# Row maxima of both heads of a pair in one product, and 64-bit weights converted with one VectorE pass

## The chip, the cores and the metric

The kernel runs on one core of a Trainium2 chip. The metric is the time of one execution in microseconds (us) on the device. A program on one core reports the time of that core. The kernel before was run three times; the median is what counts.

A core has five engines that run their own lists of instructions in order and wait for each other by semaphores: TensorE (PE, with its weight loads shown apart as PEld), VectorE (DVE), ScalarE (ACT), GpSimd (POOL) and SyncE (SP), which here only issues DMAs.

## The reference

Three layers in a row. Attention with queries averaged in pairs (4 batches, 8 heads, 1152 keys, 576 pooled queries, 64 wide):

```python
q_pool = q.reshape(B, H, S // factor, factor, D).mean(axis=3)
scores = scale * np.matmul(q_pool, k.transpose(0, 1, 3, 2))
scores = scores - np.max(scores, axis=-1, keepdims=True)
attn = np.exp(scores)
attn = attn / (np.sum(attn, axis=-1, keepdims=True) + 1e-09)
return np.matmul(attn, v).astype(np.float32)
```

Then a gated unit on 2304 tokens of 512 features, `silu(x @ w_gate) * (x @ w_val) @ w_out`, with 1536 hidden units, and a layer of eight soft experts with four slots each: a softmax of `x @ phi` over the tokens makes the slots' inputs, two layers per expert their outputs, and a softmax over the slots the result. `w_gate`, `w_val` and `w_out` arrive as 64-bit floats, all else as 32-bit floats.

## The kernel before

Attention goes in 16 steps, four batches with four pairs of heads. Of each pair the kernel forms, for every key chunk of 128 and 512 queries, the scores in a PSUM bank `st` (`unit`, lines 372 to 394): a product of `KK` and `QQ` (line 380; keys in float16 over queries in high and low float16 halves) and one of `KL` and `QH` (line 381; the keys' low halves over the queries' high ones). In two more rows of `QH` (64 and 65, against rows of 16.0 in `KL`) stand minus a query's greatest score, in a high and a low half: so the second product also takes the maximum off. ScalarE makes the exponential (line 386), GpSimd or VectorE what its high half lacks (line 393), and TensorE multiplies with the values (lines 424 to 426).

The maxima come from `row_max` (243 to 334), one head at a time: products of the high halves into banks `mx` (lines 268 and 272), and VectorE's greatest of each bank (line 288, 294, 298). In pairs 1 to 4 (`SC_STEPS`) ScalarE copies one bank of two to SBUF (280) and VectorE takes both in one scan (281) and copies its last column out (282). Then four small VectorE operations per head (300, 301, 304, 305) make the two halves. For pairs up to 6 TensorE turns them and ScalarE copies them into `QH` (327, 331, 333). From pair 7 on (`MT_STEP`) one product turns them (310), ScalarE copies them out (312), and two DMAs per head, and two more with head 1, put them in their rows (314, 320).

`split_pair` (204 to 242) makes the halves of the next pair's keys and queries and copies them by DMA to where the products want them; it is called at the start of each step for the pair of the next. `maxima` paces the row maxima: at the start of a step 18 of the 21 banks of its pair (`MXN`, `LEAD`) have been asked for, and all of head 0 must be there before the step's first scores (9), all of head 1 before its own (21).

The weights of the gated unit are converted during steps 1 to 6 (`PREP_BEG`, `PREP_END`), six pieces of 128x512 a step, 36 in all. `conv` (519 to 541) reads a 64-bit number as two words. ScalarE scales the high word as a float (532). VectorE shifts the low word (534), shifts the scaled number and joins the two (535), and joins the sign (538).

From step 4 on blocks of the gated unit (lines 602 to 607 on TensorE, 613 to 644 around it) are mixed in, three blocks are left when attention ends, and then come the experts. A scheduler sets the order on each engine, from a simulated timeline and the order of the code; what `maxima`, `prep` and `moe_work` ask for at each unit decides what it has to choose from.

Of the kernel before, what the change touches and what calls it, by code (L numbers as in the profile page):

```python
# [10 lines left out]
F16 = mybir.dt.float16  # L11
# [3 lines left out]
U32 = mybir.dt.uint32  # L15
AF = mybir.ActivationFunctionType
# [48 lines left out]
def tile_pool_attention_glu_softmoe(  # L65
# [65 lines left out]
    # places for the conversion of weights at first, for the experts' weights later  # L131
# [7 lines left out]
    # the last blocks' tokens lie apart from what is free with the attention's end  # L139
# [34 lines left out]
    def cast(what, b, p, dst, src):  # L174
        """Copies for which the scalar engine has time in the first steps."""
# [17 lines left out]
    def first_split(kd, qd, KK, KL, QQ, QH):  # L193
        """The first head with no more transfers, to begin early."""
# [9 lines left out]
    def split_pair(b, p, first=None):  # L204
# [6 lines left out]
        QH = at.tile([D + 2, 2, SQ], F16, tag="QH", bufs=2, name=f"QH{b}_{p}")  # L211
# [6 lines left out]
        # both heads of the pair at once; DMAs copy the halves to where the products want them  # L218
# [3 lines left out]
        kh = at.tile([P, S], F16, tag="kh", bufs=1, name=f"kh{b}_{p}")  # L222
        cast("k", b, p, kh[r], kr[r])
# [7 lines left out]
        heads = range(1 if first else 0, 2)  # L231
        for hd in heads:
# [10 lines left out]
    def row_max(b, p, hd):  # L243
# [12 lines left out]
        def bank():  # L256
            n_bank[0] += 1
            tg, bf = "mx", MXB
            if first and n_bank[0] % 2 or i < MX_STEPS and n_bank[0] % MX_OF == 1:
                tg, bf = "mm", MMB  # L260
            return ps(tg, [P, QT], bufs=bf, name=f"mx{b}_{p}_{hd}_{n_bank[0]}")
# [13 lines left out]
        for s in range(4):  # L275
            ts = [scores(bank(), s, c * QT, QT) for c in range(2)] if not first and i in SC_STEPS else []
            if ts:
                # while the scalar engine has time it brings a bank to SBUF, and two banks go through one scan
                w = h_tile(f"ms{b}_{p}_{hd}_{s}")[1]
                nc.scalar.copy(w, ts[0])  # L280
                nc.vector.tensor_tensor_scan(out=w, data0=ts[1], data1=w, initial=-3.0e38, op0=ALU.max, op1=ALU.max)  # L281
                nc.vector.tensor_copy(out=mp[:, s, :2], in_=w[:, QT - 1:].to_broadcast([P, 2]))
# [804 lines left out]
```

## Time and profile before

| what | before |
|---|---|
| three runs | 950.49, 954.99 and 955.86 us, median 954.99 us |
| span of the profiled execution | 951.9 us, 3.1 us below the median |
| PE busy | 843.9 us, 89% of the span |
| DVE busy | 679.5 us, 71% |
| POOL busy | 450.3 us, 47% |
| ACT busy | 365.7 us, 38% |
| DMA queue 1 | 51.5% of 16 engines |
| mean granted TensorE clock | 0.956 |

The profile is of one execution; its span runs from the first to the last instruction, and its own time is taken as that span. A busy share is a mean over stages that have different limits. So the span was cut where attention steps end (the last normalisation of a step, line 449 on five columns, begins there): 0 to 67.4 us is step 0, 67.4 to 187.9 steps 1 to 3, 187.9 to 333.2 steps 4 to 6, 333.2 to 761.4 steps 7 to 15, and the rest the last blocks and the experts. TensorE's products overlap, so its busy time is more than it would need back to back.

### The profile page before, as it was taken

The numbers are of one execution on the slowest core, as the hardware profiler recorded it, in microseconds if no ns is written. First come the engines' busy times: TensorE is split into PE (matmuls) and PEld (weight loads), VectorE is DVE, ScalarE is ACT, GpSimd is POOL, SyncE is SP. The second block draws the span as 40 slices with busy tenths as digits, with TensorE's granted clock in tenths as the row PEclk, the third lists the DMA queues.
The fourth block names the chain that finished last, engine by engine and source line by source line (L and its number), as shares of the span: only waits on it lengthen the run. The fifth ranks groups of instructions, "written<-read, shape, count | busy, mean of one in ns | idle before, by whom it ended". The sixth has DMA issues, their size and how long they took to land.

```text
span 951.9 us, 24241 instructions
## 1 busy us (share of the span) xinstructions
PE 843.9 (89%) x10071; PEld 584.5 (61%) x10071; DVE 679.5 (71%) x1266; ACT 365.7 (38%) x699; POOL 450.3 (47%) x382
## 2 busy tenths in 40 slices
PE   3887777879988779999898989998999999998897
PEld 1454454558555557767575766765777787776445
DVE  6899999998899766787867796867676343543313
ACT  2456666654555421433332434143334411212112
POOL 7555856564568830655754677265546500000100
PEclk9788998999998999999998999998999999999998
DMA  6465456564866572243523243331312189548899
GB/s 180 131 175 175 107 185 202 147 199 130 202 156 203 147 185 46 62 116 74 116 68 98 68 123 72 106 69 34 73 32 35 24 236 304 136 134 189 260 291 280
DMA packets 150070, 132.51 MB, mean 139 GB/s; under 512 B 81352, under 2 KB 118920, under 8 KB 149960
## 3 DMA queue, kind: packets, MB, share of 16 engines
q1 hardware_dynamic: 149960, 130.96, 51.5%
q8 instruction: 79, 1.29, 0.6%
q14 instruction: 31, 0.25, 0.1%
HBM read 84.10 MB, written 7.86 MB: 97 GB/s over the span
## 4 chain that ended last, share of the span: by engine, by line
PE 58%; DVE 22%; DMA 10%; issue 4%; SPq 3%; ACT 1%; POOL 0%; DVEq 0%; ACTq 0%
PE mx L268 5%; PE st L380 4%; PE st L381 4%; PE v L602 4%; PE v L607 4%; PE g L602 4%; PE v L606 4%; PE g L606 4%; PE g L607 4%; PE pv L425 2%; PE pv L424 2%; PE pv L426 2%; DVE ms L281 2%; DMA KK<-kh 2%; DVE mp L288 2%
## 5 line engine op out<-in xcount | busy, mean ns | idle before, releaser
L393 POOL TENSOR_TENSOR PL<-P 128x512 f16<-128x512 f32 (+1 forms) x295 | 330.7, 1136 | 276.2 <-ACT P L386 270.8
L386 ACT ACTIVATE P<-st 128x512 f32<-128x512 f32 (+1 forms) x336 | 189.3, 582 | 185.1 <-PE st L381 160.6
L288 DVE TENSOR_REDUCE mp<-mx 128x1 f32<-128x512 f32 x192 | 128.6, 683 | 32.4 <-PE mx L268 31.8
L268 PE MATMUL mx<-KK,QQ 128*128 128x512 f16 (+2 forms) x384 | 116.0, 353 | 39.3 <-DVE mp L288 12.3
L424 PE MATMUL pv<-VV,P 128*128 128x65 f16 x1088 | 144.6, 196 | 6.2 <-DVE x L452 6.1
L380 PE MATMUL st<-QQ,KK 128*128 128x512 f16 (+1 forms) x576 | 142.0, 297 | 5.1 <-ACT P L386 4.7
L425 PE MATMUL pv<-VV,P 128*128 128x64 f16 x1088 | 145.0, 198 | 0.0
L426 PE MATMUL pv<-VV,PL 128*128 128x65 f16 x1088 | 140.5, 195 | 1.6 <-DVE PL L393 1.5
L381 PE MATMUL st<-QH,KL 66*128 66x512 f16 (+1 forms) x576 | 140.0, 297 | 0.2
L602 PE MATMUL g<-xT,wgv 128*128 128x256 f16 x432 | 119.1, 276 | 7.1 <-DVE hs L614 6.5
L424 PEld LDWEIGHTS <-P 128*128 128x128 bf16 x1088 | 106.0, 100 | 28.3 <-issue 7.6
L602 PE MATMUL v<-xT,wgv 128*128 128x256 f16 x432 | 118.7, 275 | 0.6 <-DVE hs L616 0.5
L606 PE MATMUL g<-xT,wgv 128*128 128x256 f16 x432 | 119.0, 275 | 0.0
L607 PE MATMUL g<-xT,wgv 128*128 128x256 f16 x432 | 118.9, 275 | 0.1
L606 PE MATMUL v<-xT,wgv 128*128 128x256 f16 x432 | 118.8, 275 | 0.0
L607 PE MATMUL v<-xT,wgv 128*128 128x256 f16 x432 | 118.6, 274 | 0.0
L426 PEld LDWEIGHTS <-PL 128*128 128x128 f16 x1088 | 105.4, 101 | 20.0 <-issue 5.9
L425 PEld LDWEIGHTS <-P 128*128 128x128 bf16 x1088 | 105.3, 100 | 19.5 <-issue 6.2
L606 PEld LDWEIGHTS <-wgv 128*128 128x128 f16 x864 | 85.2, 99 | 30.1 <-issue 12.7
L602 PEld LDWEIGHTS <-wgv 128*128 128x128 f16 x864 | 85.6, 99 | 22.9 <-issue 6.2
L607 PEld LDWEIGHTS <-wgv 128*128 128x128 f16 x864 | 85.0, 99 | 18.7 <-issue 1.9
L613 ACT ACTIVATE hs<-g 128x512 f32<-128x512 f32 x54 | 32.1, 596 | 93.0 <-PE g L607 51.5
(182 smaller groups left out, 1404.3 us busy)
## 6 DMA issues: line engine op xcount, KB each, us to landing
w<-in_w SPq DMA_DIRECT2D x16, 1024.0 KB
w<-in_w SPq DMA_DIRECT2D x64, 256.0 KB
vr<-in_vP SPq DMA_DIRECT2D x16, 585.0 KB
KK<-kh SPq DMA_DIRECT2D x62, 144.0 KB
qr<-in_qT SPq DMA_DIRECT2D x15, 576.0 KB
kr<-in_kT SPq DMA_DIRECT2D x15, 576.0 KB
ro<-in_w_out SPq DMA_DIRECT2D x12, 512.0 KB
rw<-in_w_gate SPq DMA_DIRECT2D x24, 256.0 KB
```

Of the source, the lines that this page charges most:

```text
L268: nc.tensor.matmul(t, QQ[r, s * P:(s + 1) * P], KK[r, kc], start=True, stop=True)
L288: nc.vector.reduce_max(out=mp[:, s, c:c + 1], in_=t, axis=AX.X)
L380: nc.tensor.matmul(t[:, o:o + w], KK[:, k], QQ[:, q0:q0 + w], start=True, stop=False)
L381: nc.tensor.matmul(t[:, o:o + w], KL[:, k], QH[:, q0:q0 + w], start=False, stop=True)
L386: marks.append(nc.scalar.activation(P32[:, :o], t[:, :o], AF.Exp, scale=1.0 / 16.0).ins.name)
L393: eng.tensor_tensor(out=PL[:, :o], in0=P32[:, :o], in1=PH[:, :o], op=ALU.subtract)
L424: nc.tensor.matmul(dst[:, :D + 1], PH[:, q], VV[:, c, 0, :], start=first, stop=False, skip_group_check=True)
L425: nc.tensor.matmul(dst[:, :D], PH[:, q], VV[:, c, 1, :D], start=False, stop=False, skip_group_check=True)
L426: nc.tensor.matmul(dst[:, :D + 1], PL[:, q], VV[:, c, 0, :], start=False, stop=(c == NCH - 1), skip_group_check=True)
L602: mm = nc.tensor.matmul(o, w[:, 0, d, f], xh, start=(d == 0), stop=False)
L606: nc.tensor.matmul(o, w[:, 0, d, f], xl, start=False, stop=False)
L607: nc.tensor.matmul(o, w[:, 1, d, f], xh, start=False, stop=(d == ND - 1))
```

## The change

**Weights.** ScalarE does two operations per piece and VectorE one. The scaling uses the function Prelu with a slope of -2^32 for negative numbers, which leaves the sign as one more bit of the exponent; a second operation takes the top byte of the low word, divides it by 32 and writes the whole number; one VectorE pass shifts and joins. `L534` and `L538` go, a ScalarE line 546 comes.

**Row maxima.** A tile `QD` holds the high halves of a pair's queries, head 0 in rows 0 to 63 of its first half, head 1 in rows 64 to 127 of its second, zeros elsewhere. So one product of 128 columns of `QD` with the pair's keys `kh` (both heads over each other, as they were cast) gives scores of either head: nine groups of 128 queries, each every ninth column, times 1152 keys. Pair 0 keeps the way by heads (`row_max_first`). The scans are gone: every bank is one reduction. `QD` is one buffer, filled by two DMAs per pair from `qh`, and `kh` is read by the products themselves, so both can be written anew only when the last product of the pair before has read them.

**One row.** The maximum goes into one row of `QH` in one float16, and `KL` has one row of 16.0. One VectorE operation takes the greatest of nine groups at once (337), one ScalarE operation scales and rounds it (`taken_off`, 307), and one DMA of 128 rows of nine numbers writes it to `QH` (341). There are no turning products from pair 1 on, and no DMAs of `L314` and `L320`.

**Pace.** Before a step's first scores all of its pair's maxima are asked for (`MX0 + MXP * i`), and those of the next pair between 4% and 85% of the step; in step 0 from 40% to its end.

```diff
 def split_pair(b, p, first=None):
...
+        if not first:
+            for hd in heads:
+                nc.sync.dma_start(out=QD[rows[hd], hd, :], in_=qh[rows[hd], :])
...
+    def taken_off(dst, src):
+        nc.scalar.activation(dst, src, AF.Copy, scale=-1.0 / 16.0, bias=math.log(PSC))
+    NGQ = SQ // D
+    def row_max(b, p):
+        kh = KHs.pop((b, p))
+        mp = at.tile([P, NGQ, 3], F32, tag="mp", bufs=2, name=f"mp{b}_{p}")
+        R = S - 2 * QT
+        def scores(t, g, k0, kw):
+            q = QD.rearrange("p h q -> p (h q)")[:, g::NGQ]
+            nc.tensor.matmul(t, q, kh[:, k0:k0 + kw], start=True, stop=True)
+        for g in range(NGQ):
+            for c in range(2):
+                t = ps("mx", [P, QT], bufs=MXB, name=f"mx{b}_{p}_{g}_{c}")
+                scores(t, g, c * QT, QT)
+                nc.vector.reduce_max(out=mp[:, g, c:c + 1], in_=t, axis=AX.X)
+                yield
+            if g % 4 == 3 or g == NGQ - 1:
+                g0 = g // 4 * 4
+                n = g + 1 - g0
+                t = ps("mx", [P, 4, R], bufs=MXB, name=f"mx{b}_{p}_{g}_r")
+                for x in range(n):
+                    scores(t[:, x, :], g0 + x, 2 * QT, R)
+                nc.vector.reduce_max(out=mp[:, g0:g + 1, 2:3], in_=t[:, :n, :], axis=AX.X)
+                yield
+        nm = at.tile([P, NGQ], F32, tag="nm", bufs=2, name=f"nm{b}_{p}")
+        nc.vector.tensor_reduce(out=nm, in_=mp, axis=AX.X, op=ALU.max)
+        mt = at.tile([P, NGQ], F16, tag="mt", bufs=2, name=f"mt{b}_{p}")
+        taken_off(mt, nm)
+        nc.sync.dma_start(out=QHs[b, p][D:D + 1].rearrange("o h (q g) -> o (h q) g", g=NGQ), in_=mt)
+        yield
...
-        nc.scalar.mul(y, hi.bitcast(F32), sc * 2.0**-112)
+        nc.scalar.activation(y, r[:, :, 1].bitcast(F32), AF.Prelu, scale=sc * 2.0**-112, alpha=-(2.0**32))
         w = t[:, 3 * n:]
-        nc.vector.tensor_scalar(w, lo, 29, None, ALU.logical_shift_right)
+        top = r[:, :, 0].bitcast(U8)[:, :, 3]
+        nc.scalar.activation(w, top, AF.Copy, scale=1.0 / 32.0, bias=1.0 / 64.0 - 0.5)
         nc.vector.scalar_tensor_tensor(
             out=w, in0=y.bitcast(U32), scalar=3, in1=w, op0=ALU.logical_shift_left, op1=ALU.bitwise_or
         )
-        nc.vector.scalar_tensor_tensor(
-            out=w, in0=hi, scalar=1 << 31, in1=w, op0=ALU.bitwise_and, op1=ALU.bitwise_or
-        )
...
-            maxima(int(MXN * (i + f) + (LEAD if i else 9 + LEAD0 * f)))
+            if i:
+                maxima(MX0 + MXP * i + int(MXP * min(1.0, max(0.0, f - MX_BEG) / (MX_END - MX_BEG))))
+            else:
+                maxima(9 + int((MX0 - 9) * min(1.0, f / MX0_END)) + int(MXP * max(0.0, f - MX1_BEG) / (1.0 - MX1_BEG)))
```

The order that the scheduler makes of it differs in three places that matter below.

VectorE in step 1, before, while the first weights are converted (`ro` and `rw` are pieces of weights, `ms` a scan of two banks, `mp` the maxima):

```order
L535 SCALAR_TENSOR_TENSOR ro1_975<-ro1_975 128x512
L281 SCALAR_TENSOR_TENSOR ms0_2_0_1_1056<-mx0_2_0_4_1054,ms0_2_0_1_1056 128x512
L534 TENSOR_SCALAR rw0_0_1091<-rw0_0_1091 128x512
L538 SCALAR_TENSOR_TENSOR ro1_975<-ro1_975 128x512
L282 COPY mp0_2_0_1005<-ms0_2_0_1_1056 128x2
L535 SCALAR_TENSOR_TENSOR rw0_0_1091<-rw0_0_1091 128x512
L281 SCALAR_TENSOR_TENSOR ms0_2_0_2_1111<-mx0_2_0_6_1109,ms0_2_0_2_1111 128x512
L221 TENSOR_TENSOR qr1_0_1572<-qr1_0_1572 128x576
L538 SCALAR_TENSOR_TENSOR rw0_0_1091<-rw0_0_1091 128x512
L282 COPY mp0_2_0_1005<-ms0_2_0_2_1111 128x2
L281 SCALAR_TENSOR_TENSOR ms0_2_0_3_1157<-mx0_2_0_8_1155,ms0_2_0_3_1157 128x512
```

And now, in the same step:

```order
L325 TENSOR_REDUCE mp0_2_901<-mx0_2_4_0_1096 128x1
L547 SCALAR_TENSOR_TENSOR rw0_0_1056<-rw0_0_1056 128x512
L325 TENSOR_REDUCE mp0_2_901<-mx0_2_4_1_1111 128x1
L458 TENSOR_SCALAR rs0_1_0_1133<-pv0_1_0_905 128x4
L325 TENSOR_REDUCE mp0_2_901<-mx0_2_5_0_1140 128x1
L459 RECIPROCAL rs0_1_0_1133<-rs0_1_0_1133 128x4
L325 TENSOR_REDUCE mp0_2_901<-mx0_2_5_1_1150 128x1
L547 SCALAR_TENSOR_TENSOR rw0_1_1153<-rw0_1_1153 128x512
L461 TENSOR_TENSOR x320_1_0_1136<-pv0_1_0_905,rs0_1_0_1133 128x256
L325 TENSOR_REDUCE mp0_2_901<-mx0_2_6_0_1181 128x1
```

Where there stood three passes per piece and a scan with its copy, there stand one pass per piece and two reductions.

TensorE before, as it goes from step 0 to step 1 (`pv` are products with the values, `st0_1_0` the first scores of pair 1; the transposes of that pair's first maxima, `mt0_1_0`, are 26 products further up):

```order
L426 LDWEIGHTS PL0_0_15_558
L426 MATMUL pv0_0_1_502<-VV0_0_120,PL0_0_15_558 128x65
L424 LDWEIGHTS P320_0_16_583
L424 MATMUL pv0_0_1_502<-VV0_0_120,P320_0_16_583 128x65
L425 LDWEIGHTS P320_0_16_583
L425 MATMUL pv0_0_1_502<-VV0_0_120,P320_0_16_583 128x64
L268 LDWEIGHTS QQ0_1_300
L268 MATMUL mx0_1_1_6_853<-KK0_1_299,QQ0_1_300 128x512
L381 LDWEIGHTS KL1_103
L381 MATMUL st0_1_0_811<-QH0_1_301,KL1_103 128x512
```

And now, at the same place (`mx0_1_8` is the last group of pair 1's maxima, `tx` turns features of pair 0):

```order
L319 LDWEIGHTS QD_106
L319 MATMUL mx0_1_8_1_750<-kh0_1_308,QD_106 128x512
L319 LDWEIGHTS QD_106
L319 MATMUL mx0_1_8_r_771<-kh0_1_308,QD_106 128x128
L500 LDWEIGHTS xhl0_0_206
L500 MATMUL tx0_0_803<-id16_66,xhl0_0_206 64x64
L500 LDWEIGHTS xhl0_0_206
L500 MATMUL tx0_0_803<-id16_66,xhl0_0_206 64x64
L390 LDWEIGHTS KL1_103
L390 MATMUL st0_1_0_816<-QH0_1_306,KL1_103 128x512
```

The second product of the scores, which needs the row of maxima, now follows the last product of those maxima after two small ones.

SyncE before, where step 1 ends (the loads of pair 3 stand in one piece, and nothing there writes maxima):

```order
L236 DMA QQ0_3_1545<-qh0_3_1550 64x576
L237 DMA QQ0_3_1545<-ql0_3_1552 64x576
L240 DMA QH0_3_1546<-qh0_3_1550 64x576
L239 DMA KL1_103<-kl0_3_1554 64x1152
L240 DMA QH0_3_1546<-qh0_3_1550 64x576
L526 DMA ro2_1576<-in_w_out 128x1024
L526 DMA ro3_1692<-in_w_out 128x1024
L481 DMA_TRANSPOSE xT0_799<-xhl0_1_810 128x4x128
L481 DMA_TRANSPOSE xT1_801<-xhl0_1_810 128x4x128
```

And now:

```order
L247 DMA QH0_3_1484<-qh0_3_1488 64x576
L238 DMA QD_106<-qh0_3_1488 64x576 x2
L247 DMA QH0_3_1484<-qh0_3_1488 64x576
L240 DMA KK0_3_1482<-kh0_3_1486 64x1152
L341 DMA QH0_2_826<-mt0_2_1360 1x128x9
L241 DMA KK0_3_1482<-kh0_3_1486 64x1152
L240 DMA KK0_3_1482<-kh0_3_1486 64x1152
L490 DMA_TRANSPOSE xT0_799<-xhl0_1_815 128x4x128
L490 DMA_TRANSPOSE xT1_801<-xhl0_1_815 128x4x128
L241 DMA KK0_3_1482<-kh0_3_1486 64x1152
```

The DMA that writes pair 2's maxima (`QH0_2<-mt0_2`) now stands behind the two that refill `QD` for pair 3 and behind two more loads of pair 3.

## Rows read from the trace of the kernel before

**Rows 1.** The page, 40 equal slices of the span, VectorE busy in tenths.

```profile
DVE  6899999998899766787867796867676343543313
```

**Rows 2.** Windows: stretch; us; busy PE, PEld, DVE, ACT, POOL; granted clock, DMA share, GB/s.

```profile
0.00:67.40 67.40, 43.62 (x403) 23.82 (x404) 53.91 (x76) 27.02 (x46) 41.87 (x39) 0.87 0.56 155
67.40:187.90 120.50, 94.05 (x1212) 59.23 (x1210) 118.45 (x199) 76.70 (x150) 76.78 (x56) 0.92 0.55 165
187.90:333.20 145.30, 125.55 (x1494) 85.44 (x1494) 127.24 (x213) 75.80 (x144) 97.30 (x74) 0.94 0.64 174
333.20:761.40 428.20, 405.25 (x5189) 291.96 (x5188) 305.60 (x586) 150.06 (x289) 231.74 (x199) 0.98 0.32 78
761.40:951.90 190.50, 175.45 (x1778) 124.04 (x1778) 74.32 (x197) 36.09 (x71) 2.60 (x15) 0.96 0.84 229
```

**Rows 3.** Chain of waits from 67.4 to 187.9, shares by line.

```profile
by line: DVE ms L281 14.5%; issue 13.8%; DVE PL L393 7.0%; DVE mp L282 6.3%; DVE rw L535 5.1%; DVE rw L538 4.8%; PE mx L268 4.1%; DVE mm L304 3.3%; DVE nm L301 2.4%; PE st L381 2.3%; PE st L380 2.3%; DMA rw<-in_w_gate 2.3%; DVE mp L298 2.3%
```

**Rows 4.** Chain of waits from 187.9 to 333.2, shares by line.

```profile
by line: DMA KK<-kh 10.1%; DMA wo_d<-ro 5.7%; DMA rw<-in_w_val 5.3%; PE mx L268 4.8%; DVE mp L288 4.3%; DVE ro L538 4.0%; PE st L380 3.8%; issue 3.8%; DMA QH<-qh 3.6%; PE st L381 3.4%; DMA vr<-in_vP 2.8%; DMA ro<-in_w_out 2.6%; PE pv L426 2
```

**Rows 5.** Windows of line 534 alone, the first pass: VectorE busy, instructions.

```profile
67.40:187.90 120.50, 8.96 (x17) 0.92 0.55 165
187.90:333.20 145.30, 11.67 (x18) 0.94 0.64 174
```

**Rows 6.** Windows of line 538 alone, the third pass, the same stretches.

```profile
67.40:187.90 120.50, 15.07 (x17) 0.92 0.55 165
187.90:333.20 145.30, 18.48 (x18) 0.94 0.64 174
```

**Rows 7.** One line each: minimum, median and maximum ns of L534 and L538.

```profile
L534 DVE TENSOR_SCALAR rw<-rw x24: 393/420/1264, 82.6 to 321.7; 128x512 uint32<-128x512 uint32 x24
...
L538 DVE SCALAR_TENSOR_TENSOR rw<-rw x24: 660/680/1533, 86.0 to 323.6; 128x512 uint32<-128x512 uint32 x24
```

**Rows 8.** Groups by line, VectorE, row maxima: count, busy us, mean ns, idle before.

```profile
L288 DVE TENSOR_REDUCE mp<-mx 128x1 f32<-128x512 f32 x192 | 128.6, 683 | 32.4 <-PE mx L268 31.8
...
L281 DVE TENSOR_TENSOR_SCAN ms<-mx,ms 128x512 f32<-128x512 f32 x32 | 38.8, 1212 | 2.0 <-PE mx L268 1.9
...
L298 DVE TENSOR_REDUCE mp<-mx 128x1 f32<-128x384 f32 x48 | 25.9, 546 | 8.0 <-PE mx L272 7.9
...
L282 DVE COPY mp<-ms 128x2 f32<-128x2 f32 x32 | 14.4, 449 | 0.0
...
L305 DVE TENSOR_TENSOR mm<-nm,mm 128x4 f16<-128x4 f32 (+1 forms) x32 | 10.9, 341 | 0.6
...
L300 DVE TENSOR_REDUCE nm<-mp 128x4 f32<-128x12 f32 (+1 forms) x32 | 5.2, 161 | 0.6
```

**Rows 9.** Groups by line, ScalarE: scan copies and weight scaling.

```profile
L280 ACT COPY ms<-mx 128x512 f32<-128x512 f32 x32 | 18.7, 585 | 22.0 <-PE mx L268 18.2 <-DVE mm L304 2.6 <-DVE xhl L457 0.7
...
L532 ACT ACTIVATE rw<-rw 128x512 f32<-128x512 f32 x24 | 16.3, 677 | 11.3 <-DMA rw<-in_w_val 8.3 <-PE mx L268 3.0
```

**Rows 10.** Chain of waits, 460 to 475: start, us, what; end of one head's maxima.

```profile
460.95 0.48 DVE mp L298
...
463.91 0.97 DVE mm L305
...
465.18 0.26 ACT mT L312
465.46 0.67 SPq L314
...
466.18 3.05 DMA QH<-mT
...
469.73 0.22 PE st L381
```

**Rows 11.** Groups by line, weight loads of TensorE.

```profile
L424 PEld LDWEIGHTS <-P 128*128 128x128 bf16 x1088 | 106.0, 100 | 28.3 <-issue 7.6 <-DVE x L452 6.5
...
L1023 PEld LDWEIGHTS o<-soS,cTa 96*128 96x128 f32 x48 | 7.3, 231 | 2.3 <-issue 2.1 <-DVE ob L1025 0.2
```

More of the change, by code (lines that the diff above doesn't have):

```diff
@@ L158, in tile_pool_attention_glu_softmoe @@
     NKQ = 2
-    KLs = [at.tile([D + 2, 2, S], F16, name=f"KL{i}") for i in range(NKQ)]
+    KLs = [at.tile([D + 1, 2, S], F16, name=f"KL{i}") for i in range(NKQ)]
     for t in KLs:
-        nc.gpsimd.memset(t[D:D + 2, :, :], 16.0)
+        nc.gpsimd.memset(t[D:D + 1, :, :], 16.0)
+    QD = at.tile([P, 2, SQ], F16, name="QD")
+    nc.gpsimd.memset(QD[:D, 1, :], 0.0)
+    nc.gpsimd.memset(QD[D:, 0, :], 0.0)
+    KHs = {}
     def load_pair(b, p):
@@ L257, in bank @@
             n_bank[0] += 1
[L258 to L261, printed above, removed]
+            tg, bf = ("mm", MMB) if hd == 0 and n_bank[0] % 2 else ("mx", MXB)
+            return ps(tg, [P, QT], bufs=bf, name=f"mx0_{hd}_{n_bank[0]}")
         def scores(t, s, k0, kw):
@@ L266, in scores @@
                 KK, _, QQ = hs[hd][:3]
-                r = slice(0, D if first else P)
+                r = slice(0, P if hd else D)
                 nc.tensor.matmul(t, QQ[r, s * P:(s + 1) * P], KK[r, kc], start=True, stop=True)
@@ L275, in row_max @@
         for s in range(4):
[L276 to L282, printed above, removed]
-                yield
-                yield
-            else:
-                for c in range(2):
-                    t = scores(bank(), s, c * QT, QT)
-                    nc.vector.reduce_max(out=mp[:, s, c:c + 1], in_=t, axis=AX.X)
-                    yield
+            for c in range(2):
+                t = scores(bank(), s, c * QT, QT)
+                nc.vector.reduce_max(out=mp[:, s, c:c + 1], in_=t, axis=AX.X)
+                yield
         t = bank().rearrange("p (s k) -> p s k", s=4)
@@ L325, in row_max @@
-        t = ps("tr", [2, QT + 2 * REM], F16, bufs=TRB, name=f"mt{b}_{p}_{hd}")
+        nm = at.tile([P, 5], F32, tag="nm0", bufs=1, name=f"nm0_{hd}")
+        nc.vector.tensor_reduce(out=nm[:, :ns], in_=mp[:, :ns], axis=AX.X, op=ALU.max)
+        QH = QHs[0, 0]
+        t = ps("tr", [1, QT], F32, bufs=TRB, name=f"mt0_{hd}")
         for q in range(4):
-            nc.tensor.transpose(t[:, q * P:(q + 1) * P], mm[:, :, q], id16)
+            nc.tensor.transpose(t[:, q * P:(q + 1) * P], nm[:, q:q + 1], id32)
@@ new lines, in row_max_first @@
+        yield
[10 more added lines that the diff above has]
+        for g in range(NGQ):
+            for c in range(2):
+                t = ps("mx", [P, QT], bufs=MXB, name=f"mx{b}_{p}_{g}_{c}")
[15 more added lines that the diff above has]
+        nc.sync.dma_start(out=QHs[b, p][D:D + 1].rearrange("o h (q g) -> o (h q) g", g=NGQ), in_=mt)
@@ L349, in max_stream @@
     def max_stream():
-        for b, p in steps:
-            for hd in range(2):
-                yield from row_max(b, p, hd)
+        for hd in range(2):
+            yield from row_max_first(hd)
+        for b, p in steps[1:]:
+            yield from row_max(b, p)
     def maxima(n):
-        while n_rm[0] < min(n, MXN * len(steps)):
+        while n_rm[0] < min(n, MX0 + MXP * (len(steps) - 1)):
             next(maxs)
@@ L498, in attn @@
         for n, parts in enumerate(units):
-            maxima(MXN * (b * NP + p) + (MXN if parts[0][0] or parts[0][2] == QT else 9))
+            i = b * NP + p
+            maxima(MX0 + MXP * i if i or parts[0][0] or parts[0][2] == QT else 9)
             with tc.high_priority(offset=HP_U0 if b == 0 else HP_U1):
```

56 lines of the change are left out of this document (13 added, 43 removed).

## The prediction

> **What bounds the kernel now.** I read the page's slices first. VectorE is at nine tenths from the second slice to about the twelfth and falls to six or seven after the weights are converted [rows 1]; the share of 71% for the whole span hides that. So I cut the span at the ends of the attention steps [rows 2] and asked each stretch for itself what ends last. Stretch A (steps 1 to 3, 120.5 us): VectorE is busy for 118.45 us, 98%, the other engines for 64 to 78%. Its chain of waits names eight VectorE lines among its largest, 45.7% together, the scans first [rows 3]. A is bound by VectorE. Stretch B (steps 4 to 6, 145.3 us): VectorE 88%, TensorE 86%, and the chain is spread: six DMAs hold 30.1% of it, two VectorE lines 8.3% [rows 4]. B is bound by no one engine. Stretch C (steps 7 to 15, 428.2 us): TensorE 405.25 us, 95% at a granted clock of 0.98; VectorE 71%. C is bound by TensorE. The tail of 190.5 us holds none of what is changed.
>
> **The weights.** Of three passes the first (L534) and the third (L538) go. In A they hold 8.96 + 15.07 = 24.0 us of VectorE, in B 11.67 + 18.48 = 30.2 us [rows 5, 6], and one piece of 36 in step 0 some 2 us. That is the upper end: their means hold waits that may only move to the next operation. By the medians, 0.42 and 0.68 us [rows 7], a piece costs 1.1 us, 18.7 us for A's 17 pieces and 19.8 for B's 18. I take the upper end, because the operations that go are among those that wait. ScalarE gets a second operation of 0.677 us per piece [rows 9] if it costs as the first does; half or double is possible, 0.3 to 1.4. In A that is 17 x 0.677 = 11.5 us more, against 24 scan copies of 0.585 = 14.0 us less. ScalarE stays near 75 of 120.5 us. In B it is 12.2 us more on 75.80 of 145.3 [rows 2], which is hidden. A change of function table would add to this, but the order has one table load in either kernel.
>
> **The maxima.** By pair on VectorE before, with scans: 8 x (1.212 + 0.449) + 5 operations of 0.683 to 0.546 (3.0) + 2 heads x four small operations (L300, L301, L304, L305, of which first and last stand; 1.45 together) = 19.2 us; without scans 16 x 0.683 + 3.0 + 2.9 = 16.8 [rows 8]. After: 20 reductions of a full bank, 13.7 us, one of 128 columns and the greatest of 27 numbers, each between 0.161 and 0.546; I take 0.45 for both, 14.1 us. So a pair gives back 5.1 us (pairs 1 to 4) or 2.7 us. The maxima of a pair are made in the step before, so A gets 3 x 5.1 = 15.3 us, B 3 x 2.7 = 8.1, C 8 x 2.7 = 21.6, step 0 about 7.7 with pair 0's small operations. With the weights A loses 39 of its 118 us on VectorE, B 38 of 127, C 22 of 306, step 0 10 of 54.
>
> On TensorE a bank's product is spaced by 0.22 us [rows 10], so 18 of 512 and 9 of 128 columns are 4.5 us a pair, about what the old products took (16 of 512, 8 of 128, and six of 384 that lie side by side in twos), and the turning products go: half a microsecond a pair less.
>
> **What the path gets.** In A what is late next is not one engine: VectorE would have 79 us, GpSimd has 76.78, ScalarE about 75, TensorE 94.05 by busy time [rows 2]. C shows how tight this order gets: TensorE busy for 94.6% of it. A as tight as C takes 94.05 / 0.946 = 99.4 us, 21 less; bounds are 8 less (GpSimd, ScalarE and TensorE each wait for the others) and 37 less (79 us at 95%). B as tight as C takes 125.55 / 0.946 = 132.7, 13 less; bounds 4 and 20, since a third of its chain is DMAs that stay. C gets the half microsecond of eight pairs, 4 us, bounds 0 and 8. Of step 0's 10 us I count 3, as half of it is the start. Sum: 21 + 13 + 4 + 3 = 41 us less.
>
> **What it adds: a wait at each hand-over.** Before, head 0's maxima ended well ahead of a step, head 1's in its middle. Now both end together, and the second product of a step's first scores stands behind them on TensorE, which takes its list in order; behind it stand the values, the next maxima and the gated unit, and ScalarE and GpSimd wait for the scores. At the first hand-over two products of 64 columns lie between (the order shown above). I counted the products between the last of a pair's maxima and that score product at all 15 hand-overs, at 0.22 us per 512 columns [rows 10]: 0.1, 1.1, 2.7, 3.8, 4.2, 4.9, 5.0, 2.8, 5.6, 5.0, 3.9, 4.7, 6.8, 3.0 and 5.4 us of cover. The chain to be covered: product end 0.2, the two reductions 0.45, ScalarE 0.26, issue on SyncE 0.67, DMA 3.05 [rows 10] = 4.6 us. The DMA is of another form (128 pieces of 18 bytes), so 3.05 is an estimate from the nearest row. SyncE is in order too, and the row's DMA stands behind up to four others at 0.67 each: 4.6 to 7.3 us. Shortfalls over the 15 add up to 15 us for a chain of 4.6, 29 for 5.8, 46 for 7.0. Before, by the same count, some 9 us. I take a chain of about 5.2, which is 23 - 9 = 14 us more; ends 6 and 37. Refilling `QD` (it waits for the last product of the pair before, and the next pair's first product waits for it: two issues and a landing, 4.4 us) falls into the same gap and is not counted twice. Two more DMAs a pair for `QD`, and one for the row where there were none (six from pair 7 on), change SyncE's load by some 2 us a step.
>
> So 41 - 14 = 27 us less: a span of 951.9 - 27 = 925 us. The median of the runs lies 3.1 us above that span, so 928 us.
>
> [...] The stationary side of each new product is `QD` at every ninth column, 18 bytes apart. No row here shows such a load: those of float16 and bfloat16 at 2 and 4 bytes take 0.100 us and hide behind products, the slowest load on the page, float32 by rows of 96, takes 0.231 [rows 11]. [...]
>
> **The rivals.**
> *The wait decides* (slower). If the chain takes 8.2 us, as the one of rows 10 did from 460.95 to 469.23 with its VectorE queue, the shortfalls are 64 us, 55 more than before: 951.9 - 41 + 55 = 966, so 969 us. It decides from 41 / 15 = 2.7 us net per hand-over. For it: SyncE's list puts other loads ahead, some of which wait for the same products; the cover is 0.1 and 1.1 us at the first two. Against it: from pair 7 on the old chain had a DMA too, and four small operations more.
> *The next engine takes it* (no change). A gets 8, B 4, C and step 0 5, the hand-overs cost 12: 5 us less, 947, so 950 us. For it: four engines in A within 20 us of each other, each waiting for the next. Against it: in C two engines at 95% and 71% run side by side.
> *It packs* (much faster). A gets 37, B 20, C 8, step 0 5, the hand-overs cost 6: 64 less, 888, so 891 us. For it: GpSimd's and VectorE's operations also wait for each other less. Against it: B's DMAs.
> *Slow loads.* At 0.231 instead of 0.100, nine loads a pair for 128 columns (0.055 us) are uncovered by up to 0.13 us, and so is part of the other 18: 15 x 27 x 0.131 = 53 us if all count, 18 if only the nine do. I take 18: 946 us.
>
> **How the numbers follow.** Forecast 0.52, the wait decides 0.14, the next engine takes it 0.12, it packs 0.14, slow loads 0.08. About half a per cent, 4.8 us, is what a measurement of this kernel can tell from no change: faster means below 950.2, slower above 959.8. The forecast (905 to 948 by its own bounds), the packing, most of the slow loads and half of the unchanged case are faster: 0.77. Slower is the wait case, 0.14. Same is the rest, 0.09. The range goes from 893, where most of the packing case is left out, to 955, where the wait case is left out.
>
> **What would show it.** In the profile after: VectorE's total near 570 us instead of 679.5; step 3 ending near 166 instead of 187.9 us, step 6 near 300; ScalarE's new operation near 0.68 us; weight loads from `QD` at 0.10 us; TensorE waiting for the DMA `QH<-mt` at the hand-overs, 1 to 5 us each. Wrong would be: stretch A as long as before with VectorE idle, hand-overs above 5 us each, or a longer stretch C.

## The result, and the profile after

The changed kernel takes **916.87 us** (median of 4 runs, 913.64 to 921.39), the kernel before in the same session 952.74 us (948.96 to 955.86). The ratio is 0.964 (95% interval 0.9606 to 0.9675): faster by 35.9 us, where 27 were forecast. The profiled execution has a span of 917.5 us at a mean granted clock of 0.953.

VectorE by slices, against [rows 1]; it is no longer full from the second slice to the twelfth:

```profile
DVE  6868787676897356776778677666663443544223
```

The windows between the same step ends (line 458 on five columns now), columns as in [rows 2]: step 0, A, B, C, tail.

```profile
0.00:59.02 59.02, 37.37 (x394) 21.96 (x395) 44.31 (x61) 22.34 (x36) 37.33 (x39) 0.97 0.57 159
59.02:180.57 121.55, 99.28 (x1180) 65.92 (x1179) 90.19 (x152) 73.14 (x142) 77.58 (x60) 0.83 0.63 181
180.57:311.12 130.55, 118.12 (x1483) 85.18 (x1481) 93.70 (x158) 80.02 (x153) 89.85 (x72) 0.99 0.69 201
311.12:730.24 419.12, 401.71 (x5124) 295.22 (x5125) 279.08 (x519) 148.07 (x280) 230.90 (x199) 0.96 0.35 80
730.24:917.50 187.26, 172.03 (x1778) 121.02 (x1776) 74.57 (x197) 36.06 (x71) 2.52 (x15) 0.98 0.83 232
```

Read the second line first. VectorE lost 28 us of work in A, from 118.45 to 90.19, and A did not get shorter: 121.5 us against 120.5. The granted clock there fell from 0.92 to 0.83. What the kernel won it won in step 0 (8.4 us), in B (14.8), in C (9.1) and, with no change there, in the tail (3.2; over all kernels below the tail lies between 187.3 and 194.1 us, so this cannot be put down to the change).

TensorE's waits in A: who waited for what, us in total, times, longest.

```profile
PE st L390 <- DMA QH<-mt: 7.0, 2, 5.8
...
PE st L389 <- ACT P L395: 2.6, 4, 1.0
PE st L390 <- DMA KK<-kh: 2.5, 1, 2.5
...
PE mx L319 <- DMA QD<-qh: 1.3, 1, 1.3
```

VectorE waits most in A for the products whose maxima it takes, once for 5.9 us:

```profile
DVE mp L325 <- PE mx L319: 17.8, 10, 5.9
```

The first hand-over, from step 0 to step 1, in order of time (start us, us, engine, line, operation; in brackets the idle time before it and what ended it):

```profile
62.08 0.22 PE L319 MATMUL mx_r<-kh,QD 128*128 128x128 f16 x1
...
62.89 2.62 SPq L490 DMA_TRANSPOSE xT<-xhl  x2
...
63.14 0.28 DVE L334 TENSOR_REDUCE mp<-mx_r 128x1 f32<-128x128 f32 x1
63.34 0.75 DVE L182 CAST kh<-kr 128x1152 f16<-128x1152 f32 x1
64.00 0.18 DVE L337 TENSOR_REDUCE nm<-mp 128x9 f32<-128x27 f32 x1
...
64.21 0.21 ACT L307 ACTIVATE mt<-nm 128x9 f16<-128x9 f32 x1 [1.11 <-DVE nm L337]
65.60 0.55 SPq L341 DMA_DIRECT2D QH<-mt  x1
...
68.58 1.04 PE L390 MATMUL st<-QH,KL 65*128 65x512 f16 x2 [5.79 <-DMA QH<-mt]
```

After the last product of the maxima (62.08) VectorE has a reduction, a cast of the next pair and the greatest of 27; ScalarE rounds; SyncE is busy with two transposing DMAs until 65.5 and issues the row's DMA at 65.60; at 68.58 TensorE goes on, 5.8 us idle. Windows of 4 us there, columns as above: from 60 to 64 us VectorE is full and TensorE little more than half busy; from 64 to 68 TensorE does nothing, and until 72 its granted clock is 0.50.

```profile
60.00:64.00 4.00, 2.37 (x21) 1.10 (x19) 4.00 (x10) 0.94 (x3) 1.25 (x1) 0.86 0.29 100
64.00:68.00 4.00, 0.00 (x0) 0.00 (x0) 0.18 (x2) 0.21 (x1) 2.36 (x1) 0.50 0.45 85
68.00:72.00 4.00, 3.42 (x10) 1.31 (x11) 1.92 (x3) 2.25 (x4) 2.03 (x2) 0.50 0.97 221
```

The second hand-over, windows from 100 to 116 us: VectorE is full and TensorE has little before it, and just after it is the other way round. The clock is still at 0.98 from 100 to 104 us and at 0.50 from 104 on, while TensorE's wait for the row (1.17 us) ends at 106.55: here it fell ahead of that wait, after a window in which TensorE was half busy.

```profile
100.00:104.00 4.00, 1.96 (x16) 1.06 (x16) 4.00 (x8) 1.37 (x5) 3.31 (x2) 0.98 0.40 88
104.00:108.00 4.00, 2.67 (x9) 0.88 (x10) 3.78 (x8) 1.44 (x4) 1.53 (x2) 0.50 0.71 144
108.00:112.00 4.00, 4.00 (x23) 1.90 (x22) 1.38 (x2) 1.61 (x4) 2.89 (x3) 0.50 0.85 173
112.00:116.00 4.00, 4.00 (x41) 3.10 (x40) 0.69 (x1) 1.35 (x3) 1.94 (x3) 0.74 0.93 327
```

The loads of `QD` and the new ScalarE operation, one line each (minimum, median, maximum ns), against [rows 11] and [rows 9]:

```profile
L319 PEld LDWEIGHTS <-QD x405: 137/138/203, 39.4 to 691.1; 128*128 128x128 f16 x135
```

```profile
L546 ACT ACTIVATE rw<-rw x24: 638/665/712, 82.1 to 297.8; 128x512 uint32<-128x512 uint8 x24
```

### The profile page after: what moved, and what is told of

It is laid out like the page before. It is cut to its first block, busy times and chain, and to the rows that moved or that the text cites. A ratio compares the mean times of both kernels' runs of the same rounds, so it can differ in the third digit from the quotient of the medians.

```text
span 917.5 us, 23732 instructions
## 1 busy us (share of the span) xinstructions
PE 828.5 (90%) x9954; PEld 589.3 (64%) x9954; DVE 581.8 (63%) x1083; ACT 359.6 (39%) x682; POOL 438.2 (48%) x384
## 3 DMA queue, kind: packets, MB, share of 16 engines
q8 instruction: 78, 1.28, 0.6%
## 4 chain that ended last, share of the span: by engine, by line
PE 61%; DVE 7%; DMA 7%; issue 2%; POOL 2%; SPq 1%; ACT 1%; ACTq 0%; DVEq 0%; POOLq 0%
PE g L611 5%; PE g L616 5%; PE g L615 5%; PE st L389 5%; PE v L611 5%; PE st L390 5%; PE v L616 5%; PE v L615 5%; PE mx L319 4%; PE pv L433 2%; PE pv L434 2%; PE pv L435 2%; PE hp L973 2%; PE so4p L1007 1%; DMA rw<-in_w_val 1%
## 5 line engine op out<-in xcount | busy, mean ns | idle before, releaser
L402 POOL TENSOR_TENSOR PL<-P 128x512 f16<-128x512 f32 (+1 forms) x295 | 320.8, 1099 | 244.0 <-ACT P L395 241.7
L325 DVE TENSOR_REDUCE mp<-mx 128x1 f32<-128x512 f32 x270 | 179.7, 683 | 58.6 <-PE mx L319 57.5
L390 PE MATMUL st<-QH,KL 65*128 65x512 f16 (+1 forms) x576 | 147.3, 300 | 12.9 <-DMA QH<-mt 10.0
L389 PE MATMUL st<-QQ,KK 128*128 128x512 f16 (+1 forms) x576 | 145.9, 294 | 9.5 <-ACT P L395 9.0
L611 PE MATMUL g<-xT,wgv 128*128 128x256 f16 x432 | 121.0, 280 | 5.5 <-DVE hs L623 3.9
L616 PE MATMUL g<-xT,wgv 128*128 128x256 f16 x432 | 120.7, 279 | 1.1 <-POOL wgv L584 1.1
L615 PE MATMUL g<-xT,wgv 128*128 128x256 f16 x432 | 121.0, 280 | 0.0
L435 PEld LDWEIGHTS <-PL 128*128 128x128 f16 x1088 | 105.5, 101 | 15.5 <-issue 3.2
L319 PE MATMUL mx<-kh,QD 128*128 128x512 f16 x270 | 105.7, 406 | 10.4 <-DVE mp L325 6.0
L390 PEld LDWEIGHTS <-KL 65*128 65x128 f16 x576 | 52.7, 100 | 46.7 <-issue 24.8
```

What stands on the lines that cost most here:

```text
L319: nc.tensor.matmul(t, q, kh[:, k0:k0 + kw], start=True, stop=True)
L325: nc.vector.reduce_max(out=mp[:, g, c:c + 1], in_=t, axis=AX.X)
L389: nc.tensor.matmul(t[:, o:o + w], KK[:, k], QQ[:, q0:q0 + w], start=True, stop=False)
L390: nc.tensor.matmul(t[:, o:o + w], KL[:, k], QH[:, q0:q0 + w], start=False, stop=True)
L402: eng.tensor_tensor(out=PL[:, :o], in0=P32[:, :o], in1=PH[:, :o], op=ALU.subtract)
L435: nc.tensor.matmul(dst[:, :D + 1], PL[:, q], VV[:, c, 0, :], start=False, stop=(c == NCH - 1), skip_group_check=True)
```

## The experiments

Two theories stood at the start. **Hand-over**: VectorE's relief in A is real and is given away where a step's scores wait for all maxima of their pair. **The other engines**: GpSimd, ScalarE and TensorE hold A at its length anyway. Each kernel was timed beside the kernel before on its chip (943 to 963 us in single runs, medians 949.9 to 952.7). The table has the medians, the ratios and the stretches of the profiled execution, cut as above. A stretch is read from one execution of one order: e10 and e12 make the maxima of pairs 1 to 6 alike and differ by 4.3 us in A and 5.0 in B, so differences of that size between two kernels mean little. And the cut between B and C does not divide the work alike: of the gated unit's products of 256 columns (`wgv`) 267 or 268 lie in B before and in e1 and e6, 279 in the changed kernel and in e9, 327 in e2, 247 to 253 in e3, e4, e5, e7, e8 and e10 to e12. At 0.109 us each (the median from one start to the next in the changed kernel) 26 of them are 2.8 us of TensorE, so B and C are best read together.

| kernel | us | ratio (95%) | step 0 | A | B | C | tail |
|---|---|---|---|---|---|---|---|
| before | 952.7 | | 67.4 | 120.5 | 145.3 | 428.2 | 190.5 |
| changed | 916.9 | 0.964 (0.961 to 0.968) | 59.0 | 121.5 | 130.6 | 419.1 | 187.3 |
| e1 weights only | 940.3 | 0.989 (0.985 to 0.992) | 65.9 | 115.5 | 135.2 | 432.6 | 189.9 |
| e2 maxima only | 952.4 | 1.001 (0.998 to 1.005) | 58.4 | 133.9 | 160.8 | 410.7 | 188.4 |
| e3 row aside | 901.6 | 0.948 (0.945 to 0.952) | 62.2 | 101.9 | 130.6 | 418.3 | 188.0 |
| e4 filler from `kh` | 932.7 | 0.978 (0.970 to 0.985) | 58.7 | 129.7 | 130.2 | 421.4 | 193.4 |
| e5 neutral filler | 921.5 | 0.971 (0.966 to 0.976) | 58.5 | 120.3 | 128.1 | 419.7 | 191.0 |
| e6 weights, no scans | 932.4 | 0.982 (0.976 to 0.989) | 65.5 | 108.9 | 136.4 | 430.3 | 188.0 |
| e7 row by ScalarE | 923.3 | 0.973 (0.967 to 0.978) | 58.2 | 117.9 | 135.0 | 419.4 | 188.3 |
| e8 maxima first | 917.0 | 0.965 (0.960 to 0.971) | 58.4 | 118.0 | 131.2 | 421.7 | 188.1 |
| e9 by head to 3 | 917.4 | 0.963 (0.960 to 0.966) | 64.4 | 100.8 | 136.6 | 421.0 | 192.2 |
| e10 by head to 6 | 911.5 | 0.956 (0.951 to 0.960) | 62.1 | 101.1 | 135.2 | 417.9 | 194.1 |
| e11 columns in a row | 907.0 | 0.953 (0.950 to 0.956) | 58.9 | 111.4 | 129.0 | 413.1 | 192.0 |
| e12 both | 911.4 | 0.959 (0.955 to 0.963) | 63.5 | 96.8 | 130.2 | 425.1 | 193.1 |

### One half at a time

**e1**, the kernel before with the new `conv`:

```diff
-        nc.vector.tensor_scalar(w, lo, 29, None, ALU.logical_shift_right)
...
+        nc.scalar.activation(w, top, AF.Copy, scale=1.0 / 32.0, bias=1.0 / 64.0 - 0.5)
```

> The kernel before with the new conversion of the weights alone; maxima, scans and hand-overs as before. Theory 'hand-over': VectorE's relief in steps 1 to 3 was real and was given away at the new hand-overs, by TensorE's wait for the row and by the granted clock that falls behind it. There is no new hand-over here, so steps 1 to 3 fall from 120.5 us to 100 to 106 us, and the whole takes about 925 us (918 to 932). Rival 'the other engines': with VectorE relieved GpSimd, ScalarE and TensorE hold steps 1 to 3 at 115 us or more, and the whole takes 935 us or more.

The whole took 940.3 us and A 115.5: the rival's numbers. VectorE's busy time in A fell by 18 us and the stretch by 5. But what grew in its place is TensorE's wait for the scans (line 281 before, 282 in that kernel), from 6.4 to 13.6 us:

```profile
PE mx L268 <- DVE ms L281: 6.4, 8, 1.2
...
PE mx L269 <- DVE ms L282: 13.6, 9, 3.4
```

**e6** takes the scans out too (`SC_STEPS = ()`):

> The kernel before with the new conversion of the weights and without the scans: steps 1 to 4 take the maxima of each bank by a reduction, as the later steps do. VectorE has 4 x 2.4 us less, ScalarE 32 copies less. Theory: what held steps 1 to 3 at 115.5 us in the run with the new conversion alone was the scan's chain, two banks of products held through a copy on ScalarE and a scan on VectorE (TensorE waited 13.6 us for it); without it the stretch takes 100 to 108 us and the whole 925 to 932. Rival 'the other engines': GpSimd, ScalarE and TensorE hold it at 112 us or more, the whole 936 to 942.

A fell by another 6.6 us to 108.9, just above the band; the whole at 932.4 just above its own. So the scans held a part of e1's A, and GpSimd and ScalarE do not hold it at 115.

**e2**, the changed kernel with the three passes of before:

> The changed kernel with the three passes of before for the weights; maxima and hand-overs as changed. Theory 'hand-over': steps 1 to 3 lose some 15 us of VectorE work and pay the new hand-overs, so they stay at 118 us or more, with a granted clock of at most 0.90 there; the gain is in step 0 and in steps 7 to 15; the whole takes about 938 us (930 to 946). Rival 'the other engines': VectorE still binds steps 1 to 3 here, so its 15 us show and the stretch takes about 107 us; the whole about 930 us.

No faster than before, and 6 us above the theory's band: step 0 gains 9.0 us, A loses 13.4. B loses 15.5 and C gains 17.5, but 59 more of the gated unit's products than before lie in B, and B and C together gain 2.0. The two halves alone are worth 10.5 us less and 1.6 more; together they are worth 36. Over A the halves alone add up to 8 us more and together they are 1 more; over B and C it is 8 less and 24 less. The windows of A and B in e2:

```profile
58.43:192.31 133.88, 101.30 (x1183) 65.41 (x1183) 114.98 (x188) 63.43 (x122) 78.99 (x58) 0.81 0.54 155
192.31:353.11 160.80, 133.06 (x1532) 93.52 (x1532) 124.12 (x198) 72.11 (x138) 92.89 (x72) 0.94 0.63 181
```

VectorE has 115 us of work in A and takes 133.9 for it: it stands still for 19 us in a stretch that it filled before. That the weights' relief lets it catch up behind each hand-over would explain why the halves need each other; this is argued from the first of these lines and was not tried by itself.

### The wait taken away

**e3** sends the row to a tile that nothing reads, and the scores take a row of zeros (the lines that make the zeros are left out here):

```diff
...
-        nc.sync.dma_start(out=QHs[b, p][D:D + 1].rearrange("o h (q g) -> o (h q) g", g=NGQ), in_=mt)
+        nc.sync.dma_start(out=MTS[:, (b * NP + p) % 2], in_=mt)
```

> The changed kernel, but the row of maxima goes to a tile that nothing reads, and the row that the scores take is a constant zero: all maxima are still made and sent, the scores of a pair do not wait for them (the subtraction of the maxima is left out). Theory 'hand-over': the waits of TensorE for the row go, with them the falls of the granted clock behind them; steps 1 to 3 take 100 to 108 us instead of 121.6 at a clock of 0.93 or more, and the whole 885 to 897 us. Rival 'the other engines': steps 1 to 3 stay at 115 us or more and the whole at 907 us or more; only the 10 us of waits named for the row go.

A took 101.9 us at a clock of 0.93. VectorE's wait for the maxima's products went from 17.8 to 1.6 us:

```profile
62.16:164.02 101.86, 90.89 (x1177) 60.27 (x1175) 91.17 (x145) 71.34 (x140) 79.04 (x59) 0.93 0.69 201
```

```profile
DVE mp L330 <- PE mx L324: 1.6, 3, 0.9
```

The hand-overs cost A 19.7 us, B and C together 0.8 (26 of the gated unit's products moved from B to C, so the two cannot be told apart), and the whole 1.56% or 14.9 us (it ends 4.6 us above the band's upper end; step 0 gave 3.1 back). VectorE, ScalarE and GpSimd have within 2 us the same busy time as in the changed kernel's A, and A is 20 us shorter: the other engines do not hold it. TensorE's busy time fell from 99.3 to 90.9 us at the higher clock. So of the 19.7 us 10.8 are the named waits of TensorE for the row, `KK` and `QD`, and the other 8.9 may be the lower clock (0.83 against 0.93), the order of the work, or both.

### What in the hand-over costs: the clock, the chain, the order

**e4** and **e5** give TensorE idle products behind the last maxima of pairs 1 to 4, e4 of `kh`, e5 of constant tiles (e5's are shown, in part):

```diff
+        if b * NP + p <= 4:
+            with tc.high_priority(offset=300):
+                t = ps("tr", [P, 2 * P], bufs=TRB, name=f"fill{b}_{p}")
+                for x in range(40):
+                    fl = nc.tensor.matmul(t, id16, id32.bitcast(F16), start=True, stop=True)
+                    after(fl, lastmx[0])
```

> The changed kernel with 24 more products of 512 columns, whose result nobody reads, behind the last maxima of each of pairs 1 to 4, so that TensorE is busy while it would wait for the row at the first four hand-overs: 4 x 24 x 0.22 = 21 us of added work, the waits themselves stay. Theory 'hand-over, by the clock': the granted clock of steps 1 to 3 is 0.93 or more instead of 0.83, steps 1 to 3 take 105 to 114 us instead of 121.6, the whole 900 to 911 us. Theory 'hand-over, by the wait alone': the clock costs nothing, steps 1 to 3 stay within 3 us of 121.6, the whole at 914 to 922. Rival 'the other engines': the added products stand in the way, 920 to 935 us.

> The changed kernel with 40 more products of 256 columns of two constant tiles, whose result nobody reads, behind the last maxima of each of pairs 1 to 4: 4 x 40 x 0.107 = 17 us of added work on TensorE, while it would wait at the first four hand-overs. Unlike the products of the run before they read nothing that another operation waits to overwrite. Theory 'the clock': what the hand-overs cost beyond the named waits is the lower clock behind them; at a granted clock of 0.93 or more steps 1 to 3 take 105 to 113 us instead of 121.5 and the whole 902 to 911. Theory 'the serial order': the maxima must end before the next scores begin, so VectorE works alone ahead of a hand-over and stands idle behind it; TensorE's clock is only a sign of that, steps 1 to 3 take 118 to 128 us and the whole 914 to 926 at the better clock too.

e4 was a bad experiment. A took 129.7 us at a clock of 0.93 and the whole 932.7, in the band of the added products standing in the way: they read `kh`, and the next pair's cast had to wait for them (line 340, who waited for it; this names 2.9 of the 8.1 us that A is longer):

```profile
  DVE kh L182: 2.9, 2
```

In e5 the clock of A was 0.97, and A took 120.3 us, not 105 to 113; A and the whole (921.5) lie in the bands of the serial order:

```profile
58.52:178.86 120.34, 104.41 (x1339) 73.97 (x1338) 92.15 (x152) 72.96 (x142) 74.79 (x59) 0.97 0.60 179
```

So the clock, given back at this price, does not give back the time. What the lower clock (0.83 against 0.97) costs by itself stays open: of TensorE's 104.4 us busy in A 18.1 are the added products (`fill`), its own work took some 87 us instead of 99.3, and A fell by 1.2, so the added products may have cost what the clock gave. e5 does not rule the clock out.

**e7** issues the row's DMA from ScalarE (`nc.scalar.dma_start`), **e8** also gives the maxima a higher priority:

```diff
-            next(maxs)
+            with tc.high_priority(offset=100):
+                next(maxs)
```

> The changed kernel with the DMA of the row of maxima issued by ScalarE, which makes the row, instead of SyncE, where it stood behind two transposing DMAs of 2.62 us at the first hand-over. Theory 'the chain': each hand-over is some 0.5 to 1.2 us shorter; steps 1 to 3 fall by 3 to 6 us and the whole to 907 to 913. Theory 'the serial order': the time between VectorE's last maximum and the first score product is a small part of what the hand-over costs; the whole stays at 913 to 921.

> As the run with the row by ScalarE, and the maxima have a higher priority in the order, so that they end earlier: at the first five hand-overs 0.7, 3.7, 5.0, 8.1 and 18.6 us of other products lie between a pair's last maxima and the score product that waits for them, instead of 0.1, 1.1, 2.7, 3.8 and 4.2. Theory 'the serial order': steps 1 to 3 fall to 107 to 114 us and the whole to 898 to 908. Rival: what the maxima gain the scores of the running step lose, 912 to 922.

e7 shortened A by 3.6 us, as the theory of the chain had it, and lost 4.7 in B and C; the whole is 923.3, above both bands and no gain. In e8 TensorE's named waits for the row in A fell from 7.0 to 2.0 us:

```profile
PE st L391 <- DMA QH<-mt: 2.0, 2, 1.5
```

A was still 118.0 and the whole 917.0: the rival. So shortening the chain, or putting more products into its cover, did not bring the 20 us of e3: all of a pair's maxima still have to lie ahead of its first score. But e8 may also hold back the running step's scores, as its rival has it, so it does not price the order by itself.

### Undoing the one wait for both heads

**e9** and **e10** make the maxima of pairs 1 to 3 and 1 to 6 head by head, so that a head's scores wait for that head alone:

```diff
-        for hd in range(2):
-            yield from row_max_first(hd)
-        for b, p in steps[1:]:
+        for b, p in steps[:ONE + 1]:
+            for hd in range(2):
+                yield from row_max_one(b, p, hd)
+        for b, p in steps[ONE + 1:]:
             yield from row_max(b, p)
```

> The changed kernel, but the maxima of pairs 1 to 3 are made head by head from the float16 halves of keys and queries, with reductions and no scans, and turned into the one float16 row by products and ScalarE as those of the first pair are; pairs 4 to 15 keep the product of both heads and the row by DMA. So in steps 1 to 3 a head's scores wait for that head's maxima alone. Theory 'the serial order': steps 1 to 3 take 105 to 112 us (108.9 in the run of the weights without scans) instead of 121.5, steps 4 to 15 stay within 4 us of the changed kernel's 549.7, step 0 gives back up to 6 us; the whole 903 to 912. Rival: one of these stretches gives back what the other gains, as the operations of a head by itself cost VectorE four small ones and TensorE float32 turns; 915 to 922.

> As the run before, with the maxima of pairs 1 to 6 made head by head. Theory: in steps 4 to 6 the new kernel's hand-overs have covers of 3.8 to 4.9 us and cost little, so there head by head gains nothing: those steps take 130 to 136 us (130.6 changed, 136.4 head by head without scans), and the whole is 0 to 5 us above the run before. Rival: the serial order costs in steps 4 to 6 too, they fall to 122 to 127 us, and the whole is 4 to 8 us below the run before.

In these pairs the row's DMA, `QD` and its loads go too. In e9 A took 100.8 us with every maximum made and taken off, at a clock of 0.97:

```profile
64.40:165.16 100.76, 88.52 (x1205) 59.09 (x1205) 87.22 (x156) 72.28 (x141) 68.76 (x55) 0.97 0.67 194
```

With e3, which leaves all of that in place and takes away the wait alone, this settles what holds A: the one wait for both heads, at some 20 us of the stretch. Part of e9's 20.7 only moved across the cut: step 0 gave back 5.4 us, and 22 exponentials of 512 columns lie in it instead of 18, so four banks of step 1's scores were done before A begins. Up to the end of A e9 is 15.4 us shorter than the changed kernel, e3 16.6. B was 6.0 longer and the tail 4.9; e9's whole is 917.4, as the rival had it. With pairs 1 to 6 by head the whole is 911.5; B is 135.2, where the theory had it, but the whole is 5.9 below e9, where the rival had it. In the profiled executions 2.3 us of that lie in step 0 and 4.5 in B and C together. Why B is longer than in the changed kernel is open.

### The loads of every ninth column

**e11** reads 128 columns in a row:

```diff
-            q = QD.rearrange("p h q -> p (h q)")[:, g::NGQ]
+            q = QD.rearrange("p h q -> p (h q)")[:, g * P:(g + 1) * P]
```

> The changed kernel with the stationary side of the maxima's product read as 128 columns in a row instead of every ninth one (the maxima then come to other queries' places in the row, which leaves that part of the computation wrong; all work and transfers stay). The loads fall from 138 to 100 ns, 405 x 38 ns = 15 us of loads. Theory 'hidden': the loads lie beside the products of 128 and 512 columns, and the whole stays within 5 us of the changed kernel's 917. Rival 'slow loads': the loads of the 128-column products (0.055 us) are not hidden, and the whole falls by 7 us or more.

```profile
L319 PEld LDWEIGHTS <-QD x405: 94/98/292, 39.4 to 673.3; 128*128 128x128 f16 x135
```

The loads fell from 138 to 98 ns and the whole to 907.0 us, 1.1% below the changed kernel with intervals that do not meet: the whole is in the rival's band. Its reason is borne out in small part only. In C, by the starts of TensorE's products, the next product follows one of `QD`'s 128 columns after 0.061 us (median), and after 0.055 in e11; it follows one of 512 columns after 0.240 us, and after 0.216 in e11. Over the 216 products of C this adds up to 3.5 us, where the loads by themselves are 216 x 40 ns = 8.6 us shorter: most of a slow load is hidden. C lost 6.0 us and B 1.5, with 32 of the gated unit's products moved from B to C. A lost 10.1 us, but there the scheduler also made another order (0.9, 3.5 and 4.1 us of cover at the first three hand-overs instead of 0.1, 1.1 and 2.7). So how much of the 9.9 us is the loads and how much the order is not shown.

**e12** was to have both exactly, with pairs 1 to 6 by head and `QD` laid out in groups by strided GpSimd copies in place of two DMAs (the lines for `QD`'s shape and for the heads are left out):

```diff
...
-                nc.sync.dma_start(out=QD[rows[hd], hd, :], in_=qh[rows[hd], :])
+                nc.gpsimd.tensor_copy(out=QD[rows[hd], :, hd * D:(hd + 1) * D], in_=qh[rows[hd], :].rearrange("p (j g) -> p g j", g=SQ // D))
```

> Both findings in one exact kernel: the maxima of pairs 1 to 6 head by head, and for pairs 7 to 15 the stationary tile laid out so that each group's 128 columns lie in a row (64 queries of either head), written from the queries by two strided GpSimd copies a pair in place of two DMAs; which queries make up a group, and so the row's DMA, stay. Theory 'both add': against the 911.5 of the run with pairs 1 to 6 by head, steps 7 to 15 lose the 4 to 8 us that the loads of every ninth column cost; stretch C 410 to 414 us instead of 417.9, the whole 903 to 909. Rival: the strided copies cost GpSimd 1 us or more each and hold back its subtractions and the first product of a pair, the whole at 911 or more.

The whole was 911.4, no better than e10. The loads were at 97 ns, but C took 425.1 us, 7.2 more than in e10. C holds as many of the gated unit's products in both. The copies are long, the rival's condition, and VectorE's busy time in C rose from 279.3 to 287.5 us with the same work:

```profile
L239 POOL COPY QD<-qh x18: 1202/1430/1777, 221.8 to 638.2; 64x576 f16<-64x576 f16 x18
```

## Why the prediction was right in its sum and wrong in its places

**The sum.** 928 was forecast, 916.9 measured, inside the range and inside the forecast case's own bounds. One sum of the working is off: with the covers listed there, a chain of 5.2 us leaves shortfalls of 21 us, not 23, so its own terms give 926 us. The span fell by 34.4 us, 7.4 more than the 27 of the working. In part the sum came out by luck: A did not get shorter at all, and step 0, C and the tail gave 13.7 us more than forecast. By stretch:

| term | forecast | measured |
|---|---|---|
| A, without the hand-overs | -21 | -18.6 (e3), -19.7 (e9) |
| B | -13 | -14.8 |
| C | -4 | -9.1 |
| step 0 | -3 | -8.4 |
| hand-overs (e3) | +14 over all 15 | +19.7 in A, +0.8 in B and C, -3.1 in step 0 |
| tail | 0 | -3.2 |

**A and its tightness** was right: with the wait gone A takes 101.9 or 100.8 us where 99.4 was worked out from C. VectorE's relief there was 28 us, not the 39 counted: the weights' three passes of 38.3 us became one of 18.9, so 19.4 us went, near the 18.7 of the medians and not the 24 that was taken, and other work (two more casts of keys) came into the stretch. What the prediction named as a sign of being wrong, stretch A as long as before with VectorE idle, came true all the same, because of the next term.

**The hand-overs** were the right mechanism in the wrong shape. Without any wait the working gives 951.9 - 41 - 9 = 902 us; e3's span is 900.9. But the prediction spread the shortfalls of a chain of 5.2 us over 15 hand-overs, with 1 to 5 us of wait at each, and the runs put them into A. Of the 15, TensorE has a named wait for the row at six, 10.0 us in all and 5.8 at the first; in A the hand-overs cost 19.7 us, where the named waits for the row, `KK` and `QD` add up to 10.8. The step that failed is that a hand-over costs the wait that is seen there. It also sets all of VectorE's maxima ahead of all of the next scores: the windows at the first two hand-overs show VectorE full while TensorE has little to do, and then TensorE late, at a granted clock of 0.50, while VectorE has little to do (1.92 and 1.38 of 4 us from 68 and 108 us). How the 8.9 us beyond the named waits divide between this order and the clock is not shown (e5, e8). Four hand-overs lie in A. In B and C, with covers of 2.8 to 6.8 us and the gated unit's products to do, eleven cost 0.8 us together.

**Step 3 ending near 166, step 6 near 300**: 180.6 and 311.1; without the wait 164.0 and 294.6.

**C and step 0** were under-sized. In C TensorE's busy time fell by 3.6 us, as the half microsecond a pair had it (some 1 us of this is work of the gated unit that now lies in B), and its idle time by 5.5, from 22.9 to 17.4, which was not counted. In step 0 3 of the 10 us of VectorE work were counted, and the step fell by 8.4; no run shows that this work is the whole reason.

**Prices.** ScalarE's new operation takes 0.665 us (0.677 forecast), and either kernel has one load of a function table, of 1.28 us. VectorE's total is 581.8 us, not 570. `QD`'s loads take 138 ns, not 100; "slow loads" was given 0.08 and 18 us as a case of its own, at 231 ns. It was not a case beside the forecast but a cost within it: 3.5 us in C by the starts of the products, at most the 9.9 us of e11 in all. The row's DMA lands 2.9 us after its issue (median of 15, up to 5.1), where 3.05 was taken. The 231 ns were the author's estimate, from a load of another form; with the columns in a row (e11) the loads of `QD` take 98 ns.

**The next engine** was put at no change for the whole; e3 rules it out for A, where the other engines have the same busy time in 20 us less.

## What to carry to other kernels

Before two results are joined into one transfer, ask what each of them released by itself: one wait for both heads cost a stretch 20 us, nearly twice what its named waits showed. It lined up two engines one behind the other, and TensorE's granted clock fell there too, from 0.92 to 0.83; which of the two costs the rest was not separated. Price a freed engine and the new wait in the same stretch, and look for work that can stand in the gap; where there was some and the cover was longer (B and C), the same wait was nearly free. Where work can move across the ends of a stretch, count it on both sides before the stretch's time is read. Two halves that each bring little alone (10 us and none) can bring 36 together, so a half should not be judged by itself.

## What the runs showed of the hardware

- A weight load of 128 float16 columns that lie 18 bytes apart took 138 ns (median of 405), in a row 98 ns (e11). Of the 40 ns between them most was hidden: in C the next product's start came 24 ns later behind a product of 512 columns and 6 ns later behind one of 128.
- Two transposing DMAs held SyncE's list for 2.62 us; a row's DMA that was ready at 64.42 us went out at 65.60.
- TensorE's granted clock was 0.50 in the 4-us windows from 64 to 72 and 104 to 112 us, each time after a window in which it had been about half busy (2.37 and 1.96 of 4 us) at a granted clock of 0.86 and 0.98; with idle products there (e5) A's mean clock was 0.97, without them 0.83.
- A GpSimd copy of 64x576 float16 with a step of 18 bytes in its source took 1.43 us (median of 18, 1.20 to 1.78; e12).
